# Narrowing the float64 weights: the middle bits as integers from ScalarE, sign and exponent placed in the upper half words by VectorE, the two added as integers by GpSimd

## The chip, the cores and the metric

One NeuronCore of a Trainium2 chip. TensorE (PE in the profile; PEld is its weight load) multiplies matrices into PSUM, VectorE (DVE), ScalarE (ACT) and GpSimd (POOL) work elementwise, SyncE (SP) issues the DMAs. The metric is the device time of one execution in microseconds, lower is better.

## The reference

Attention with four sink positions and a window of 128, in 4 batches of 8 heads, then a token mixer of rank 32 and a feed-forward network (FFN) with 2048 hidden units:

```python
keep = is_sink | in_window
scores = np.where(keep, scale * np.matmul(q, k.transpose(0, 1, 3, 2)), -1e9)
a = np.exp(scores - np.max(scores, axis=-1, keepdims=True))
a = a / (np.sum(a, axis=-1, keepdims=True) + 1e-09)
x = np.matmul(a, v)                      # then (B, H, S, D) -> (B, S, H * D)
u = x + (x.transpose(0, 2, 1) @ U @ V).transpose(0, 2, 1)
return u + np.maximum(u @ w_ch1, 0.0) @ w_ch2
```

q, k and v are float32 when they are multiplied. U, V, `w_ch1` and `w_ch2` reach the kernel as float64, 8 bytes an element, and have to be made float32 on the chip: 35 blocks of 128 partitions, one of 192 columns (U), two of 384 (V) and 32 of 512 (16 slices f of the hidden units, each with one block of `w_ch1` and one of `w_ch2`).

## The kernel before

A batch is attended in pairs of heads and halves of the sequence (`attend`): scores on PE (line 598), minimum and mask on DVE (605), exponential on ACT (608), normalisation on POOL or ACT, transposes (650), masked copies, values (680). The mixer follows (`mix_half`, `mix_end`): transposes (779), a product that shrinks to rank 32 (788), its copy `t` on ACT with a correction on DVE (829), then products that go back (842), whose results DVE adds to `xT` (844); `uh` and `ul` are the high and low part of the result, as the FFN reads them.

The FFN (`ffn`) takes one half of a batch, c, and a list of slices f. One step of it is 12 products of 384 columns (lines 868 to 870), the ReLU on ACT (876), its low part `hl` on DVE (879) and 9 products of 512 columns (889). Four batches of two halves and 16 slices make 128 steps. Batch 0 goes through the slices in groups of four, each for one half and then for the other (`spread`), since the slices are narrowed on the way; attention of the next batch is mixed into each batch's FFN.

`narrow` makes one block float32. A raw block `raw` (tile `big`, a ring of four that the FFN's outputs use too) is loaded by DMA. `narrow_steps` then takes, per element, the top 16 bits (`top`) and the 32 bits below (`mid`). Line 90 or 91 (DVE or ACT) drops the sign, 92 clamps the exponent, 93 or 94 (DVE or ACT) shifts it to that of float32, 95 puts the sign back: `a` is the upper half of the float32, read as bfloat16. Line 96 keeps sign and exponent in `s`, 97 multiplies `mid` by 2^-36 and by `s`, 98 adds the two. For the weights, 97 and 98 write a PSUM bank (`BANKED`), which releases the raw block after line 97. `weights` then copies the sum to the rounded high part of `w` (lines 458 and 459, ACT or DVE) and takes the rest as the low part (465, DVE alone when banked). A step of the FFN needs all four parts of its slice.

`Plan` decides order and engine of all of this before the program is written: steps with several `ways` are given an engine by a forward pass over assumed costs and due times, in which work of DVE and POOL that is marked to use their common port excludes each other. The result is one fixed order for each engine, and each engine takes its instructions in that order and waits at the one whose operand is not there.

Of the kernel before, what the change touches and what calls it, by code (L numbers as in the profile page):

```python
# [21 lines left out]
P = 128  # L22
# [28 lines left out]
NNR = 6  # L51
# [11 lines left out]
BANKED = True  # L63
# [7 lines left out]
def f32(ap):  # L71
    return ap.bitcast(F32)
# [6 lines left out]
def narrow_steps(nc, raw, n, a, s, x=None):  # L79


    x = x or (lambda: f32(raw())[:, 1:2 * n + 1:2])
# [16 lines left out]
          "POOL": lambda: g.tensor_tensor(x(), ab(), x(), ALU.add)}, "a", "raw"),  # L99
    ]  # L100
# [314 lines left out]
def dve(n):  # L415
    return 0.069 + n * 1.042e-3
# [14 lines left out]
class Fast:  # L431
# [44 lines left out]
    def narrow(self, src, n, prio, dst=()):  # L476

        raw, A, S_ = self.raw(), self.nr(), self.nr()
        if len(self.early) > 0:
            self.early.pop(0)  # L480
        else:
            self.put(raw, lambda: (raw().bitcast(U16)[:, 1:4 * n + 1], src), P * n * 8, prio - 8.0)
        x = self.bank() if dst else None
        box = {"raw": raw, "a": A, "s": S_}
        cost = (0.069 + n * 0.52e-3, 0.069 + n * 0.26e-3, 0.069 + n * 0.26e-3, dve(n), 0.069 + n * 0.26e-3, dve(n), dve(n))
        steps = narrow_steps(self.nc, raw, n, lambda: A()[:, :n], lambda: S_()[:, :n], x and (lambda: x()[:, :n]))
        for i, ((ways, r, w), c) in enumerate(zip(steps, cost)):
            r, w = (box[r],) if r else (), box[w]
            if x and i >= 5:
                r, w = r + (w,), x  # L490
                if i == 5:
                    r += tuple(dst)
                else:
                    ways = {"DVE": ways["DVE"]}
            self.plan.any({e: (c if e == "DVE" else gps(n) if e == "POOL" else act(n) + 0.09, fn, e != "ACT" and not (x and i == 6))
                           for e, fn in ways.items()}, r=r, w=(w,), prio=prio)
        if x:
            return x, lambda: x()[:, :n]
        return raw, lambda: f32(raw())[:, 1:2 * n + 1:2]
# [33 lines left out]
    def weights(self, f, prio):  # L533

        if f in STREAMED:
            i, w = self.slot()
            self.held[f] = (i, w)
            self.recent.append(f)
        else:
            w = self.w[f] = Box(lambda i=len(self.w): self.wtiles[i])  # L540
        for j, src in enumerate((self.w1[f], self.w2[f])):
            tb, tw = self.narrow(src, DM, prio, ((w, 2 * j), (w, 2 * j + 1)) if BANKED else ())
            hi, lo = (lambda i=i: w()[:, i, :] for i in (2 * j, 2 * j + 1))
            self.copy(DM, hi, tw, psum=BANKED, r=(tb,), w=((w, 2 * j),), prio=prio)
            self.tt(DM, lo, tw, lambda hi=hi: f32(hi()), ALU.subtract, pool=not BANKED,
                    r=(tb, (w, 2 * j)), w=((w, 2 * j + 1),), prio=prio)
        if f in STREAMED:
            wd = self.wd[f]
            self.put(wd, lambda: (f32(wd()), f32(w())), 1 << 20, prio, r=(w,))
        return w  # L550
# [398 lines left out]
    def run(self):  # L949
# [8 lines left out]
        self.wtiles, self.banks, self.bigs, self.accs, tiles = [], [], list(self.early), [], []  # L958
        bigs = Ring(NBIG, None)
        self.raw, self.big = self.share(bigs, self.bigs, lambda t: t), self.share(bigs, self.bigs, lambda t: f32(t[:, :DM]))  # L960
        self.nr = ring(NNR, [P, DM], U16, "nr")
        flat = [list(pair) for pair in self.first]
# [54 lines left out]
        for i in range(NP):  # L1017
            tiles.append(self.pool.tile([P, 2, NBLK, SW + SW], F32, name=f"p{i}"))
        with tc.manual_schedule():
            for s in order:  # L1020
                s.fn()
# [240 lines left out]
```

## Time and profile before

| | |
|---|---|
| runs shown | 756.87, 757.01, 757.60 us, median 757.01 us |
| profiled execution | 756.17 us, its span 754.4 us |
| PE busy | 728.8 us, 97% of the span |
| DVE busy | 387.6 us, 51% |
| ACT busy | 319.1 us, 42% |
| POOL busy | 125.9 us, 17% |
| mean granted TensorE clock | 0.994 of full speed |

Busy shares are means over the whole span. Matmuls overlap in the records, so that a PE that is 97% busy may still run below its rate; the 40 slices, the tables by stretch and the start times of equal steps tell more. Everything of the narrowing lies before 240 us.

### The profile page before, as it was taken

How to read it: one execution, taken by the hardware profiler on the slowest of the kernel's cores; microseconds unless marked ns; L12 is line 12 of the kernel's file. 1: busy time of each engine (PE TensorE's matmuls, PEld its weight loads, DVE VectorE, ACT ScalarE, POOL GpSimd, SP SyncE). 2: the span in 40 equal slices, each digit the busy share in tenths (PEclk: the TensorE clock that was granted, in tenths of full speed). 3: DMA queues.
4: the chain of work that ended last, by engine and by line, in shares of the span. 5: the costliest groups of instructions: out<-in, count | busy, mean ns of one | idle time of the engine just before them, and what ended most of it. 6: DMA issues, size and time to landing. Idle time of an engine off the chain costs nothing.

```text
span 754.4 us, 11107 instructions
## 1 busy us (share of the span) xinstructions
PE 728.8 (97%) x4004; PEld 604.8 (80%) x4004; DVE 387.6 (51%) x1044; ACT 319.1 (42%) x898; POOL 125.9 (17%) x194
## 2 busy tenths in 40 slices
PE   7987899999999999999999999999999999999996
PEld 5556777778787887787899977877889999999995
DVE  7999899898999524235551163242651131112111
ACT  6876475774863436245521164362641111111110
POOL 4742020321312122023120030120310000000000
PEclk9999999999999999999999999999999999999999
DMA  8565767666684366542465446431256527524752
GB/s 280 167 204 206 280 233 237 244 223 231 215 297 165 126 208 209 188 176 74 159 212 197 163 156 215 168 112 56 94 176 239 214 92 263 185 106 132 261 186 94
DMA packets 39103, 140.41 MB, mean 186 GB/s; under 512 B 4352, under 2 KB 8064, under 8 KB 29568
## 3 DMA queue, kind: packets, MB, share of 16 engines
q1 hardware_dynamic: 38752, 139.23, 52.7%
q8 instruction: 33, 0.54, 0.3%
q10 hardware_dynamic: 288, 0.39, 0.2%
q14 instruction: 30, 0.25, 0.1%
HBM read 109.98 MB, written 29.62 MB: 185 GB/s over the span
## 4 chain that ended last, share of the span: by engine, by line
PE 77%; DVE 16%; ACT 3%; issue 1%; DMA 1%; DVEq 0%; ACTq 0%; SPq 0%
PE bank L889 31%; PE bank L868 11%; PE bank L869 10%; PE bank L870 10%; PE bank L598 5%; PE bank L680 3%; DVE nr L95 2%; PE bank L650 2%; DVE bank L97 2%; DVE p L605 2%; DVE w L465 1%; DVE oph L656 1%; ACT p L608 1%; DVE xT L844 1%; DVE bank L98 1%
## 5 line engine op out<-in xcount | busy, mean ns | idle before, releaser
L889 PE MATMUL bank<-w,hh 128*128 128x512 f32 x768 | 244.3, 399 | 1.9 <-DVE w L465 1.3
L879 DVE SCALAR_TENSOR_TENSOR hl<-bank,hh 128x384 fp32r<-128x384 f32 x128 | 71.1, 555 | 270.5 <-ACT hh L876 270.0
L876 ACT ACTIVATE hh<-bank 128x384 fp32r<-128x384 f32 x125 | 61.4, 491 | 277.8 <-PE bank L870 277.2
L868 PE MATMUL bank<-ul,w 128*128 128x384 f32 x512 | 177.7, 347 | 1.1 <-ACT w L458 0.3
L869 PE MATMUL bank<-uh,w 128*128 128x384 f32 x512 | 172.3, 337 | 0.7 <-DVE w L465 0.7
L870 PE MATMUL bank<-uh,w 128*128 128x384 f32 x512 | 172.1, 336 | 0.0
L889 PEld LDWEIGHTS bank<-w,hh 128*128 128x128 f32 x768 | 140.1, 189 | 30.8 <-issue 5.7
L889 PE MATMUL bank<-w,hl 128*128 128x512 f32 x384 | 152.2, 396 | 1.6 <-DVE hl L879 1.6
L868 PEld LDWEIGHTS bank<-ul,w 128*128 128x128 f32 x512 | 96.0, 188 | 19.2 <-issue 10.8
L608 ACT ACTIVATE p<-p,mn 128x260 f32<-128x260 f32 (+1 forms) x192 | 92.8, 486 | 25.9 <-DVE mn L605 24.6
L869 PEld LDWEIGHTS bank<-uh,w 128*128 128x128 f32 x512 | 96.2, 188 | 6.9 <-DVE w L465 1.8
L870 PEld LDWEIGHTS bank<-uh,w 128*128 128x128 f32 x512 | 96.1, 188 | 0.0
L889 PEld LDWEIGHTS bank<-w,hl 128*128 128x128 f32 x384 | 72.5, 189 | 18.6 <-DVE hl L879 3.1
L605 DVE CUSTOM_DVE_ANT_0 p<-bank,mask 128x260 f32<-128x260 f32 (+1 forms) x192 | 68.2, 401 | 23.7 <-PE bank L598 23.3
L467 POOL TENSOR_TENSOR p<-p 128x256 f32<-128x256 f32 (+1 forms) x34 | 29.3, 871 | 218.1 <-ACT p L608 215.6
L598 PE MATMUL bank<-kp,qp 64*128 64x260 f32 (+1 forms) x360 | 55.4, 405 | 2.3 <-DVE p L465 1.2
L598 PEld LDWEIGHTS bank<-kp,qp 64*128 64x128 f32 x360 | 30.3, 188 | 19.7 <-DVE mn L605 10.6
L680 PE MATMUL bank<-oph,vp 128*64 128x256 f32 (+1 forms) x448 | 45.4, 340 | 0.0
L680 PEld LDWEIGHTS bank<-oph,vp 128*64 128x64 f32 x448 | 28.4, 136 | 18.0 <-issue 6.9
L467 POOL TENSOR_TENSOR ul<-xT,uh 128x384 fp32r<-128x384 f32 x15 | 15.6, 1062 | 159.0 <-ACT uh L458 113.5
L660 POOL TENSOR_SCALAR_AFFINE_SELECT oph<-oph 128x384 f32<-128x384 f32 x64 | 34.0, 550 | 36.7 <-ACT oph L458 36.4
L608 ACT ACTIVATION_READ_ACCUMULATOR p<-p,mn 128x1 f32 x192 | 36.4, 190 | 0.0
(144 smaller groups left out, 697.7 us busy)
## 6 DMA issues: line engine op xcount, KB each, us to landing
w<-wd SPq DMA_DIRECT2D x60, 1024.0 KB, 4.8
big<-in_w_dram SPq DMA_DIRECT2D x32, 512.0 KB, 4.2
wd<-w SPq DMA_DIRECT2D x14, 1024.0 KB, 4.4
big<-xd SPq DMA_DIRECT2D x33, 256.0 KB, 2.8
out_dram<-big SPq DMA_DIRECT2D x24, 256.0 KB, 2.1
kp<-in_k_dram SPq DMA_DIRECT2D x12, 396.0 KB, 3.3
qp<-in_q_dram SPq DMA_DIRECT2D x12, 384.0 KB, 4.3
vp<-in_v_dram SPq DMA_DIRECT2D x12, 384.0 KB, 4.0
```

Source lines behind the costliest of these rows:

```text
L467: ways["POOL"] = (gps(n), lambda: nc.gpsimd.tensor_tensor(dst(), a(), b(), op), True)
L598: nc.tensor.matmul(st()[:, :wd], qr()[rows, q0:q0 + P], kr()[rows, k0:k0 + wd], start=True, stop=True)
L605: add("DVE", dve(wd), lambda st=st, row=row, at=at, lo=lo, wd=wd, qb=qb: nc.vector.tensor_tensor_reduce(row(), st()[:, :wd], self.mask[:, ...
L608: add("ACT", act(wd) + 0.22, lambda row=row, at=at: nc.scalar.activation(row(), row(), AF.Exp, bias=at(mn), scale=-1.0, accum_out=at(sm)), ...
L660: add("POOL", 0.126 + CH * 0.914e-3, lambda: nc.gpsimd.affine_select(top(), top(), [[0, NBLK], [1, P]], ALU.is_ge, 0.0, base=0, channel_mu ...
L680: nc.tensor.matmul(pa()[i * D:(i + 1) * D, c0 * P:(c0 + hi - lo) * P], vr()[:, i, kb - kb0, :], mv, start=n == 0, stop=n == len(mms) - 1, ...
L868: nc.tensor.matmul(ph()[:, :CH], wh, ul()[:, d, :], start=d == 0, stop=False)
L869: nc.tensor.matmul(ph()[:, :CH], wl, uh()[:, d, :], start=False, stop=False)
L870: nc.tensor.matmul(ph()[:, :CH], wh, uh()[:, d, :], start=False, stop=d == NC - 1)
L876: self.plan.any({"ACT": (act(CH), lambda: nc.scalar.activation(hh(), ph()[:, :CH], AF.Relu)), "DVE": (dve(CH), lambda: nc.vector.tensor_sc ...
L879: add("DVE", dve(CH), lambda: nc.vector.scalar_tensor_tensor(hl(), ph()[:, :CH], 0.0, f32(hh()), ALU.max, ALU.subtract), r=(ph, hh), w=(hl ...
L889: nc.tensor.matmul(acc[k](), a()[:, sl], w()[:, m, :], start=not begin and i == 0 and j == 0, stop=i == n - 1 and j == 2)
```

## The change

The weights, U and V are narrowed by `join_steps`. The steps that drop the sign, clamp and shift the exponent stay (new lines 112 to 117). The middle 32 bits are turned into a rounded integer by ACT alone (new line 114, in place in the raw block), line 118 writes sign and exponent into the upper halves of 32-bit words of a new tile `nt`, whose lower halves are zero from the start (two memsets), and POOL alone adds the two as 32-bit integers (line 119) into the raw block: its words are then the float32. Lines 96 to 98 are gone. The PSUM bank is no longer used, so that the high part is now copied from the raw block, and the low part may be taken by POOL as well as by DVE; the raw block is released only after that. `nr` has two buffers and not six, `nt` has two.

```diff
-NNR = 6
+NNR = 2
+NNT = 2
-BANKED = True
+def join_steps(nc, raw, n, a, t):
+
+    x = lambda: words(raw())[:, 1:2 * n + 1:2]
+    mid = lambda: raw().bitcast(U32)[:, 1:2 * n + 1:2]
+    top = lambda: raw().bitcast(U16)[:, 4:4 * n + 4:4]
+    topb = lambda: raw().bitcast(BF16)[:, 4:4 * n + 4:4]
+    ab = lambda: a().bitcast(BF16)
+    high = lambda: t().bitcast(U16)[:, 1:2 * n:2]
+    v = nc.vector
+    return [
+        {"DVE": lambda: v.tensor_scalar(a(), top(), 0x7FFF, None, ALU.bitwise_and),
+          "ACT": lambda: nc.scalar.activation(ab(), topb(), AF.Abs)},
+        {"ACT": lambda: nc.scalar.activation(x(), mid(), AF.Copy, scale=2.0 ** -13)},
+        {"DVE": lambda: v.tensor_scalar(ab(), ab(), TOP_MIN, TOP_MAX, ALU.max, ALU.min)},
+        {"DVE": lambda: v.tensor_scalar(a(), a(), 14336.0, 8.0, ALU.subtract, ALU.mult),
+          "ACT": lambda: nc.scalar.activation(a(), a(), AF.Copy, bias=-114688.0, scale=8.0)},
+        {"DVE": lambda: v.scalar_tensor_tensor(high(), top(), 0x8000, a(), ALU.bitwise_and, ALU.bitwise_or)},
+        {"POOL": lambda: nc.gpsimd.tensor_tensor(x(), words(t())[:, :n], x(), ALU.add)},
     ]
...
     def narrow(self, src, n, prio, dst=()):
-        raw, A, S_ = self.raw(), self.nr(), self.nr()
+        raw, A, T = self.raw(), self.nr(), self.nt()
...
+        top, mid = (raw, "t"), (raw, "m")
+        steps = join_steps(self.nc, raw, n, lambda: A()[:, :n], T)
+        use = (((top,), A), ((), mid), ((), A), ((), A), ((top, A), T), ((T,), mid))
...
-            tb, tw = self.narrow(src, DM, prio, ((w, 2 * j), (w, 2 * j + 1)) if BANKED else ())
+            tb, tw = self.narrow(src, DM, prio)
             hi, lo = (lambda i=i: w()[:, i, :] for i in (2 * j, 2 * j + 1))
-            self.copy(DM, hi, tw, psum=BANKED, r=(tb,), w=((w, 2 * j),), prio=prio)
-            self.tt(DM, lo, tw, lambda hi=hi: f32(hi()), ALU.subtract, pool=not BANKED,
+            self.copy(DM, hi, tw, r=(tb,), w=((w, 2 * j),), prio=prio)
+            self.tt(DM, lo, tw, lambda hi=hi: f32(hi()), ALU.subtract,
                     r=(tb, (w, 2 * j)), w=((w, 2 * j + 1),), prio=prio)
...
+            for t in joins:
+                nc.gpsimd.memset(t, 0)
```

The plan gives every engine another order. Over the whole program PE and SP have the same instructions as before. On DVE the instructions of lines 96, 97 and 98 (35, 35 and 34) are gone, that of line 95 is line 118 now, and of the 32 low parts of `w` 25 are left. ACT has 35 of line 114, POOL 35 of line 119 and 7 low parts of `w`.

On DVE, just ahead of the correction of the mixer's `t` (line 829 before, 840 now; `pst` is a small product of the mixer, `w0` and `w2` the first slices, `big` raw blocks, `nr` and `nt` their halves), there stood these; ten more of line 92 to 98 and others stood above them, back to the row of `pst`:

```order
L465 TENSOR_TENSOR w0_166<-bank2_160,w0_166 128x512
L92 TENSOR_SCALAR nr_770<-nr_770 128x512
L97 SCALAR_TENSOR_TENSOR bank6_164<-big0_89,nr_768 128x512
L93 TENSOR_SCALAR nr_770<-nr_770 128x512
L98 TENSOR_TENSOR bank6_164<-nr_751,bank6_164 128x512
L95 SCALAR_TENSOR_TENSOR nr_770<-big1_91,nr_770 128x512
L96 TENSOR_SCALAR nr_800<-nr_770 128x512
L465 TENSOR_TENSOR w0_166<-bank6_164,w0_166 128x512
L97 SCALAR_TENSOR_TENSOR bank7_165<-big1_91,nr_800 128x512
L92 TENSOR_SCALAR nr_802<-nr_802 128x512
L98 TENSOR_TENSOR bank7_165<-nr_770,bank7_165 128x512
L829 TENSOR_TENSOR t_807<-bank4_162,t_807 32x512
```

Now there stand only these between the row of `pst` (line 830) and the correction:

```order
L115 TENSOR_SCALAR nr_732<-nr_732 128x512
L485 TENSOR_TENSOR vst_436<-big2_93,vst_436 32x384
L118 SCALAR_TENSOR_TENSOR nt0_175<-big0_89,nr_716 128x512
L485 TENSOR_TENSOR xhl_757<-bank3_161,xhl_757 64x384
L118 SCALAR_TENSOR_TENSOR nt1_176<-big1_91,nr_732 128x512
L485 TENSOR_TENSOR w0_166<-big3_95,w0_166 128x512
L485 TENSOR_TENSOR w0_166<-big0_89,w0_166 128x512
L115 TENSOR_SCALAR nr_796<-nr_796 128x512
L116 TENSOR_SCALAR nr_796<-nr_796 128x512
L840 TENSOR_TENSOR t_798<-bank6_164,t_798 32x512
```

The work ahead of the correction has become half as many instructions, and the low parts of `w0` read the raw block in SBUF where they read a PSUM bank.

On POOL, from the last masked copy of batch 0's attention (`oph`) to the low parts of the mixer's result (`ul`), there stood:

```order
L660 AFFINE_SELECT oph_657<-oph_657 128x3x128
L660 AFFINE_SELECT oph_704<-oph_704 128x3x128
L660 AFFINE_SELECT oph_707<-oph_707 128x3x128
L467 TENSOR_TENSOR ul_839<-xT_380,uh_830 128x384
L467 TENSOR_TENSOR ul_849<-xT_380,uh_837 128x384
```

In the same place there stands now:

```order
L671 AFFINE_SELECT oph_712<-oph_712 128x3x128
L119 TENSOR_TENSOR big2_93<-nt0_175,big2_93 128x384
L119 TENSOR_TENSOR big3_95<-nt1_176,big3_95 128x512
L119 TENSOR_TENSOR big0_89<-nt0_175,big0_89 128x512
L119 TENSOR_TENSOR big1_91<-nt1_176,big1_91 128x512
L487 TENSOR_TENSOR w2_168<-big1_91,w2_168 128x512
L487 TENSOR_TENSOR ul_827<-xT_351,uh_818 128x384
L487 TENSOR_TENSOR ul_839<-xT_351,uh_825 128x384
L119 TENSOR_TENSOR big2_93<-nt0_175,big2_93 128x512
```

Four integer additions and one low part of `w2` have come between, and more follow behind the two rows of `ul`.

On ACT, between the mixer's `t` and the first ReLU (line 876 before, 887 now), the eight copies to `uh` stood in one piece, behind one instruction of line 94 and one copy to `w2`. Now five copies to `uh` stand higher up and one behind the ReLU, and directly ahead of the ReLU there are:

```order
L114 ACTIVATE big3_95<-big3_95 128x512
L478 CAST uh_818<-xT_427 128x384
L113 ACTIVATE nr_861<-big0_89 128x512
L478 CAST uh_818<-xT_494 128x384
L114 ACTIVATE big0_89<-big0_89 128x512
L117 ACTIVATE nr_832<-nr_832 128x512
L887 ACTIVATE hh_882<-bank3_161 128x384
```

The conversions of `mid` to integers stand among the copies that the FFN's first products read.

## Rows read from the trace of the kernel before

**Rows 1.** The page: span, busy by engine, DVE in 40 equal slices (tenths).
```profile
span 754.4 us, 11107 instructions
PE 728.8 (97%) x4004; PEld 604.8 (80%) x4004; DVE 387.6 (51%) x1044; ACT 319.1 (42%) x898; POOL 125.9 (17%) x194
DVE  7999899898999524235551163242651131112111
```
**Rows 2.** By stretch: its length, then busy PE, PEld, DVE, ACT, POOL; clock; DMA.
```profile
20.00:40.00 20.00, 18.12 (x135) 11.92 (x133) 19.58 (x76) 18.34 (x70) 14.68 (x22) 1.00 0.57 189
...
40.00:68.10 28.10, 21.77 (x135) 13.97 (x131) 26.72 (x58) 20.08 (x53) 8.88 (x13) 1.00 0.70 233
68.10:90.00 21.90, 19.11 (x87) 15.36 (x88) 19.84 (x37) 10.59 (x20) 3.50 (x3) 1.00 0.54 189
...
40.00:240.00 200.00, 187.57 (x1036) 146.82 (x1033) 183.22 (x437) 127.01 (x327) 42.46 (x57) 0.99 0.66 229
240.00:754.00 514.00, 508.32 (x2754) 434.86 (x2753) 169.92 (x454) 160.38 (x454) 60.02 (x93) 1.00 0.47 166
```
**Rows 3.** Line 868 alone by stretch: 128 products of it are 32 FFN steps.
```profile
68.10:257.20 189.10, 45.40 (x128) 24.20 (x129) 0.99 0.63 222
257.20:435.00 177.80, 44.58 (x128) 24.00 (x128) 1.00 0.50 174
435.00:614.00 179.00, 44.77 (x128) 23.99 (x128) 1.00 0.43 151
```
**Rows 4.** The chain that ended last, 37.6 to 86 us, by line.
```profile
by line: DVE nr L95 13.9%; DVE bank L97 9.5%; DVE w L465 8.0%; DVE xT L844 7.7%; DVE nr L96 6.6%; DVE oph L656 5.9%; ACT nr L94 5.3%; DVE ul L465 5.2%; DVE bank L98 4.2%; DVE p L605 4.2%; DVE nr L92 3.8%; issue 3.4%; DVE big L98 2.8%; DVE v
```
**Rows 5.** DVE's groups by form: total busy us, mean ns of one, idle before.
```profile
L95 DVE SCALAR_TENSOR_TENSOR nr<-big,nr 128x512 uint16<-128x512 uint16 x32 | 24.0, 751 | 1.0
L97 DVE SCALAR_TENSOR_TENSOR bank<-big,nr 128x512 f32<-128x512 uint32 x32 | 22.2, 694 | 0.6
L98 DVE TENSOR_TENSOR bank<-nr,bank 128x512 f32<-128x512 bf16 x32 | 22.0, 689 | 0.3
L465 DVE TENSOR_TENSOR w<-bank,w 128x512 fp32r<-128x512 f32 x32 | 21.9, 683 | 2.7 <-ACT w L458 2.6
L96 DVE TENSOR_SCALAR nr<-nr 128x512 uint16<-128x512 uint16 x32 | 10.0, 311 | 0.3
```
**Rows 6.** ACT's groups by form.
```profile
L91 ACT ACTIVATE nr<-big 128x512 bf16<-128x512 bf16 x27 | 18.3, 676 | 4.6 <-DMA big<-in_w_dram 4.6
L458 ACT CAST w<-bank 128x512 fp32r<-128x512 f32 x31 | 18.2, 587 | 17.7 <-DVE bank L98 17.6
L94 ACT ACTIVATE nr<-nr 128x512 uint16<-128x512 uint16 x23 | 14.5, 631 | 24.6 <-DVE nr L92 24.6
```
**Rows 7.** POOL's groups by form that are nearest to the new addition.
```profile
L467 POOL TENSOR_TENSOR xhl<-first1q,xhl 128x512 fp32r<-128x512 f32 x3 | 3.9, 1294 | 25.1 <-ACT xhl L458 10.2 <-PE bank L801 8.5 <-DVE xhl L459 6.4
...
L99 POOL TENSOR_TENSOR big<-nr,big 128x192 f32<-128x192 bf16 x1 | 0.6, 556 | 0.0
```
**Rows 8.** ACT's timeline: the first and the fourth ReLU of the FFN.
```profile
71.61 0.49 ACT L876 ACTIVATE hh<-bank 128x384 fp32r<-128x384 f32 x1 [1.82 <-PE bank L870]
...
88.06 0.49 ACT L876 ACTIVATE hh<-bank 128x384 fp32r<-128x384 f32 x1
```
**Rows 9.** The chain in order of time: two FFN steps where PE waits for nothing.
```profile
589.36 2.06 PE bank L889 x9
593.51 2.06 PE bank L889 x9
```
**Rows 10.** POOL's timeline at 228 us: start, length, what.
```profile
228.68 2.97 POOL L467 TENSOR_TENSOR vsh<-first1k,vsh 32x512 fp32r<-32x512 f32 x2 [5.47 <-ACT vsh L458]
```
**Rows 11.** DVE's timeline beside it, and one instruction where POOL is idle.
```profile
228.71 1.80 DVE L95 SCALAR_TENSOR_TENSOR nr<-big,nr 128x512 uint16<-128x512 uint16 x1
...
255.00 0.56 DVE L465 TENSOR_TENSOR ul<-xT,uh 128x384 fp32r<-128x384 f32 x1
```

More of the change, by code (lines that the diff above doesn't have):

```diff
@@ L76, in words, with narrow_steps @@
     return ap.bitcast(I32)
-def narrow_steps(nc, raw, n, a, s, x=None):
-    x = x or (lambda: f32(raw())[:, 1:2 * n + 1:2])
+def narrow_steps(nc, raw, n, a, s):
+    x = lambda: f32(raw())[:, 1:2 * n + 1:2]
     mid = lambda: raw().bitcast(U32)[:, 1:2 * n + 1:2]
@@ L99, in narrow_steps @@
           "POOL": lambda: g.tensor_tensor(x(), ab(), x(), ALU.add)}, "a", "raw"),
+    ]
+def join_steps(nc, raw, n, a, t):
[15 more added lines that the diff above has]
+        {"POOL": lambda: nc.gpsimd.tensor_tensor(x(), words(t())[:, :n], x(), ALU.add)},
     ]
@@ L482, in narrow @@
             self.put(raw, lambda: (raw().bitcast(U16)[:, 1:4 * n + 1], src), P * n * 8, prio - 8.0)
[L483 to L495, printed above, removed]
+        top, mid = (raw, "t"), (raw, "m")
+        steps = join_steps(self.nc, raw, n, lambda: A()[:, :n], T)
+        use = (((top,), A), ((), mid), ((), A), ((), A), ((top, A), T), ((T,), mid))
+        cost = (0.069 + n * 0.52e-3, 0.0, 0.069 + n * 0.26e-3, 0.069 + n * 0.26e-3, dve(n), 0.0)
+        for ways, (r, w), c in zip(steps, use, cost):
+            self.plan.any({e: (c if e == "DVE" else gps(n) if e == "POOL" else act(n) + 0.09, fn, e != "ACT")
                            for e, fn in ways.items()}, r=r, w=(w,), prio=prio)
-        if x:
-            return x, lambda: x()[:, :n]
-        return raw, lambda: f32(raw())[:, 1:2 * n + 1:2]
+        return (raw, "m"), lambda: f32(raw())[:, 1:2 * n + 1:2]
     def mixers(self):
@@ L957, in run @@
         self.t = ring(2, [P, DM], F32R, "t")
-        self.wtiles, self.banks, self.bigs, self.accs, tiles = [], [], list(self.early), [], []
+        self.wtiles, self.banks, self.bigs, self.accs, tiles, joins = [], [], list(self.early), [], [], []
         bigs = Ring(NBIG, None)
@@ L961, in run @@
         self.nr = ring(NNR, [P, DM], U16, "nr")
+        self.nt = self.share(Ring(NNT, None), joins, lambda t: t)
         flat = [list(pair) for pair in self.first]
@@ L1018, in run @@
             tiles.append(self.pool.tile([P, 2, NBLK, SW + SW], F32, name=f"p{i}"))
+        joins += [self.pool.tile([P, DM], I32, name=f"nt{i}") for i in range(NNT)]
         with tc.manual_schedule():
+            for t in joins:
+                nc.gpsimd.memset(t, 0)
             for s in order:
```

## The prediction

> **What bounds the kernel now.** The page comes first: PE is busy 97% of the span and DVE 51%, but the slices show DVE at 9 tenths in the first third and at 1 to 3 later [rows 1]. So the share of the whole says nothing of the part where the weights are narrowed. The table by stretch puts it in numbers: from 40 to 240 us DVE is busy 183.2 of 200, ACT 127.0, POOL 42.5; after 240 us DVE 169.9 of 514 [rows 2]. All narrowing lies in that first stretch.
>
> Since busy PE may be slow PE, I take equal work instead. Thirty-two FFN steps are 128 products of line 868. Those of batch 0, with attention of batch 1 between them, take 189.1 us; those of batches 1 and 2, each with the attention of one batch between them, 177.8 and 179.0, mean 178.4 [rows 3]. The other difference is the narrowing. So 10.7 us are lost inside batch 0's FFN, and that is most of what a better narrowing can return there; about 1.4 of it I set aside for six products of 512 columns that only batch 0's FFN has (0.23 each, 2.06 over 9 in [rows 9]), which leaves 9.3.
>
> Where are they? An FFN step that waits for nothing takes 4.15 us (593.51 less 589.36) [rows 9]. The first and the fourth ReLU of batch 0 are 16.45 us apart, three steps, which are 12.45 at that rate [rows 8]. So 4.0 us go in the first burst, and 5.3 in the other three groups of slices. The third place is ahead of the FFN. The chain that ended last runs on DVE almost without a break from 37.6 to 86 us, and the narrowing's lines 95, 97, 96 and 98 lead it with the mixer's own additions (844) among them [rows 4]: the FFN, which starts at 68.1, waits for a mixer that stands in DVE's queue behind the narrowing.
>
> **The change, part by part.** *DVE.* Lines 96, 97 and 98 go: 10.0 + 22.2 + 22.0 = 54.2 us for the 32 blocks [rows 5]. Line 118 costs what 95 does; it writes every second half word, which no row shows, and I take line 95's price, which is near the 0.69 of lines 97 and 98 (its 24.0 us over 32 include some delayed ones); bounds 0.6 and 0.9. Of 32 low parts 25 stay (less 4.8). DVE gets nine more exponent shifts at about 0.3, five copies to `w` and five ReLUs, at most 0.7 each: about 8. Together DVE has some 51 us less to do, 183 becomes about 132.
>
> *ACT.* 32 conversions of `mid`. The nearest rows are ACT's other passes over such a block: 0.631 from line 94, 0.676 from line 91 with a strided source [rows 6]. I take 0.65, bounds 0.55 (the step when they follow each other closely) and 0.75. That is 21 us, less nine shifts (5.7) and ten copies and ReLUs that DVE takes (about 5.4), with the smaller blocks about 11 more: 127 becomes 138 of 200. That alone bounds nothing.
>
> *POOL.* 35 integer additions and 7 low parts. The nearest row is a subtraction of 512 columns at 1.294; 192 columns of the old line 99, in the same strided block, took 0.556, which by columns gives the same [rows 7]. An integer addition is not in the trace: bounds 0.9 and 2.0, and I take 1.29. 32 + 7 at 1.29 and 2.4 for the three smaller ones are 53 us: 42.5 becomes 95 of 200. The two memsets stand ahead of POOL's first work, which waits for DVE's masks anyway.
>
> *The price that comes with it.* DVE's instruction of line 95 that started at 228.71 took 1.80 us. POOL's pair began at 228.68 and its first ended 1.28 later; DVE came to its end 0.55 us after that [rows 10, 11]. A subtraction of `ul` took 0.56 where POOL did nothing [rows 11]. So a DVE instruction that works in SBUF alone waits until POOL's is over. Those that read PSUM (97, 98, 465 as it was) kept to 0.69 throughout. The change removes just the unaffected ones and doubles POOL's time. About 145 such DVE instructions are left before 240 us (32 times the clamp, line 118 and most low parts, 21 shifts, some 40 of mixer and attention). At a POOL busy 95 of 200 us, nearly every second meets one, and half of about 1 us is lost each time: some 35 us. DVE ends near 132 + 35 = 167, still under 183.
>
> This is what the Trainium skill, "GPSIMD Engine Reference", section 8 (Key points), says: VectorE and GpSimd share SBUF interfaces, and instructions with two SBUF inputs or in a two-port mode contend. The low part of `w` had one SBUF input and has two now, so that by this rule the change moves work from the free kind to the contending one; the trace agrees (0.56 against 1.80 with POOL busy).
>
> *Moved work.* Between `pst` and the correction of `t`, DVE had 21 instructions, 14 of the kinds at 0.55 to 0.7 and 7 at 0.3, some 11 us by [rows 5]; the new order has nine, 6 and 3, some 5 us. The 6 us don't all come back, since `t` itself is made by ACT: ACT is busy 20.1 of the 28.1 us from 40 to 68.1 [rows 2]. Ahead of that the first conversions lengthen a stretch in which it has no room, 18.3 of 20 us [rows 2]. In all, by the first ReLU it has six conversions of 512 columns and three smaller ones more, about 5, less a few copies: 4 of its 8 idle us are filled. Half of what is left I give to the start of the FFN: 2.5 us earlier, bounds 0 and 5.
>
> *First burst.* At the first `hl` five blocks have passed line 118, where four had passed 95; three are left for three steps. In the time that DVE's SBUF work and POOL have to share, one block costs 0.3 (clamp) + 0.17 (shift, in 18 of 32) + 0.69 (line 118) + 0.54 (low part, in 25) + 0.08 (copy, in 6) on DVE and 1.29 + 0.28 on POOL, together 3.05 us, and with a meeting's loss of 0.3 some 3.35. Three blocks are 10 us, within the 12.45 of three steps. So the burst should lose little: 3.5 of 4.0 come back.
>
> *The other groups.* 24 blocks in the remaining 167 us are 7 us each, but they come in bursts, since a slot of `w` comes free only as an old slice has been used, and raw blocks are held until the low part is taken instead of until line 97. At 3.35 a block against steps of 5.9 us (189.1 over 32) for two blocks, the shared time is a little too short where blocks are wanted in a row, and there is room elsewhere. I take half of 5.3: 2.7 back.
>
> *Sum.* 2.5 + 3.5 + 2.7 = 8.7 us off the profiled 756.17 us: 747.5. The median of the runs is 757.01, 0.84 above that execution, so 748.3.
>
> **Rivals.** *A, the FFN starts no earlier and ACT is the next to be late.* The conversions now stand among the copies to `uh` that the first products read, and ACT is over 9 tenths busy in batch 0's attention [rows 2]. Against: 8 idle us before the FFN. Then only the bursts gain, 3 to 4 us: 753.
>
> *B, nothing is won.* The low part now needs ACT's conversion, POOL's addition and ACT's copy in turn, with `nr` and `nt` two deep and the raw block held longer. If each block takes as long as the 3.5 us that DVE needed (0.75 + 0.31 + 0.69 + 0.69 + 0.68 by [rows 5], some 0.4 for clamp and shift), the wait for line 98 becomes one for 119: 757.
>
> *C, slower: DVE stands still behind POOL.* In the shared time alone 32 blocks at 3.35 are 107 us where 32 of clamp, line 95 and line 96 were about 45; with POOL's 42 and some 20 of other DVE work that is 169 of 200. It decides when DVE is held during more than 51 of POOL's 95 us, over half; then DVE's 132 is above 183 again. At three quarters it is 71, 20 too many, of which PE would see about half, since its own steps cover the rest: 767. For it: the order is fixed, so that a held DVE also holds masks and `hl`. Against: line 95 took 0.75 on average with POOL busy a fifth of the time, only 9% over its own. The rule of the Trainium skill just named would lead here if every addition met a DVE instruction.
>
> *D, all is won:* 9.3 and 5, so 743.
>
> **Chances.** The forecast, 748 (745 to 751), 0.45; D 0.08; A 0.20; B 0.09; C 0.18. The range of 8 in 10 goes from D to B's upper end, 742 to 758, and leaves out C and little else. The likeliest case's own range is the 745 to 751 given with it. Within 0.2% (1.5 us, about what this kernel's runs can tell apart) lies B and a bit of A: same 0.10; faster 0.45 + 0.08 + 0.19 = 0.72; slower 0.18.
>
> **What the profile of the changed kernel would show.** Right: 128 products of line 868 in batch 0 in about 183 us; the first at 65 to 66; the first to fourth ReLU in 13 us; DVE 20 to 50 us less busy in all, POOL near 179, ACT near 330; POOL's addition at 1.2 to 1.4 us. The chain from 40 to 86 should show ACT and POOL beside DVE. Wrong: line 118 or the low part of `w` at a mean of 1 us or more (C); PE waiting for POOL's line 119 or ACT's copies of `w` in the bursts (B); the first product of the FFN at 68 or later (A). An addition of 2 us would make a block 4.1 us of shared time and turn the sum round.

## The result, and the profile of the changed kernel

The changed kernel takes 749.17 us (median of 4 runs, 748.03 to 750.35) against 756.94 us beside it: ratio 0.99, 95% interval 0.9877 to 0.9924. It is 7.8 us faster; 8.7 had been forecast. Its profiled execution took 748.03 us, with a span of 746.3, 8.1 less than the span in [rows 1].

The page: span, busy time by engine and DVE's 40 slices.

```profile
span 746.3 us, 11090 instructions
...
PE 725.6 (97%) x4004; PEld 604.3 (81%) x4004; DVE 357.1 (48%) x949; ACT 326.8 (44%) x910; POOL 182.8 (24%) x242
...
DVE  7889787776886614426541253243651131112112
```

The table by stretch, columns as in [rows 2]:

```profile
40.00:240.00 200.00, 191.48 (x1082) 153.42 (x1081) 160.99 (x358) 137.82 (x347) 98.04 (x101) 1.00 0.68 239
240.00:746.00 506.00, 500.91 (x2717) 428.12 (x2715) 164.46 (x445) 157.25 (x447) 58.87 (x92) 1.00 0.47 166
```

DVE went from 183.2 to 161.0 of 200 us and POOL from 42.5 to 98.0, and nearly all that changed lies ahead of 250 us. Line 879 (868 before), 128 products to a row, answers to [rows 3]:

```profile
66.10:249.80 183.70, 44.79 (x128) 24.03 (x129) 1.00 0.65 229
249.80:427.60 177.80, 44.58 (x128) 24.00 (x128) 1.00 0.49 174
427.60:606.70 179.10, 44.81 (x129) 24.01 (x128) 1.00 0.43 151
```

The first product comes at 66.1 instead of 68.1, batch 0's FFN takes 183.7 instead of 189.1, the other batches take what they took. That is 7.4 of the 8.1 us; another 0.8 lie behind the last step of batch 2 and were not followed.

Inside batch 0's FFN I now cut where the fifth step's first product starts. Before, then after the change, all engines by stretch:

```profile
68.10:87.80 19.70, 16.91 (x75) 13.24 (x76) 18.69 (x35) 9.88 (x19) 3.50 (x3) 1.00 0.50 174
87.80:257.20 169.40, 166.09 (x912) 135.09 (x912) 146.35 (x360) 102.22 (x268) 32.13 (x44) 0.99 0.64 227
```

```profile
66.10:86.00 19.90, 15.71 (x76) 13.16 (x76) 17.18 (x24) 12.12 (x24) 8.31 (x6) 1.00 0.58 187
86.00:249.80 163.80, 162.77 (x913) 134.06 (x912) 123.41 (x296) 106.93 (x274) 73.18 (x76) 1.00 0.66 235
```

PE does the same work in each pair (75 or 76 instructions, then 912 or 913), so the lengths can be compared. The first four steps won nothing: 19.7 before, 19.9 after. PE stands still for 4.2 us of them, where it stood still for 2.8 before; its busy time fell by 1.2 us at the same clock, for a reason that no row shows. The other 28 won 5.6 us, and PE stands still in them for only 1.0 us. The ReLUs of [rows 8] say the same of the first burst, 16.25 us between them instead of 16.45:

```profile
70.04 0.47 ACT L887 ACTIVATE hh<-bank 128x384 fp32r<-128x384 f32 x1
...
86.29 0.49 ACT L887 ACTIVATE hh<-bank 128x384 fp32r<-128x384 f32 x1 [2.49 <-PE bank L881]
```

The new and the kept groups by form (busy us, mean ns, idle before):

```profile
L119 POOL TENSOR_TENSOR big<-nt,big 128x512 int32<-128x512 int32 x32 | 43.6, 1364 | 57.1 <-DVE nt L118 45.3 <-ACT nr L113 6.1 <-DMA big<-in_w_dram 2.2
L118 DVE SCALAR_TENSOR_TENSOR nt<-big,nr 128x512 uint16<-128x512 uint16 x32 | 25.6, 802 | 2.3 <-ACT nr L117 1.4 <-issue 0.6
L485 DVE TENSOR_TENSOR w<-big,w 128x512 fp32r<-128x512 f32 x25 | 22.8, 914 | 1.6 <-ACT w L478 1.6
L115 DVE TENSOR_SCALAR nr<-nr 128x512 bf16<-128x512 bf16 x32 | 14.3, 450 | 6.8 <-ACT nr L113 6.7
```

The low part of `w` rose from 0.683 [rows 5] to 0.914 us and the clamp takes 0.450: DVE does stand behind POOL, though for less time than was reckoned.

Last, PE's standstills of more than 0.15 us in the first four steps, from its timeline (start, length, operation, in brackets the idle time and who ended it):

```profile
68.61 0.44 PE L879 MATMUL bank<-ul,w 128*128 128x384 f32 x1 [0.72 <-DVE ul L485]
...
76.22 0.51 PE L900 MATMUL bank<-w,hl 128*128 128x512 f32 x1 [2.19 <-DVE hl L890]
...
81.37 0.73 PE L900 MATMUL bank<-w,hh 128*128 128x512 f32 x2 [1.18 <-ACT hh L887]
```

DVE's timeline has what stood ahead of the `hl` that ended the longest:

```profile
71.32 1.29 DVE L115 TENSOR_SCALAR nr<-nr 128x512 bf16<-128x512 bf16 x1
72.54 1.67 DVE L485 TENSOR_TENSOR ul<-xT,uh 128x384 fp32r<-128x384 f32 x1
...
75.62 0.55 DVE L890 SCALAR_TENSOR_TENSOR hl<-bank,hh 128x384 fp32r<-128x384 f32 x1
```

The ReLU for that `hl` had ended at 72.4. DVE came to it at 75.6, after six others, among them a clamp of 1.29 us and a `ul` of 1.67 that take 0.29 and 0.55 where POOL is idle. There is another candidate in the same stretch. ACT's timeline has the copy of the fourth block:

```profile
70.41 0.65 ACT L478 CAST w<-big 128x512 fp32r<-128x512 f32 x1
```

The chain that ended last goes on from it to POOL's low part and a load:

```profile
71.14 1.33 POOL w L487
...
72.49 4.54 DMA big<-in_w_dram
```

That copy starts at 70.41, though POOL's sum was done at 68.14; only when POOL has taken the low part does the raw block come free, and the load that waits for it lands at 77.0. The last of the three standstills leads to the same load: the third ReLU stands on ACT behind lines 113, 114 and 117 of the block that it brings, and line 117 waits 1.38 us for a clamp that DVE makes at 79.99, behind a low part of 1.70 us.

### The profile page after: what moved, and what is told of

Same layout as the page of the kernel before. It is cut to its first block, busy times and chain, and to the rows that moved or that the text cites. A ratio compares the mean times of both kernels' runs of the same rounds, so it can differ in the third digit from the quotient of the medians.

```text
span 746.3 us, 11090 instructions
## 1 busy us (share of the span) xinstructions
PE 725.6 (97%) x4004; PEld 604.3 (81%) x4004; DVE 357.1 (48%) x949; ACT 326.8 (44%) x910; POOL 182.8 (24%) x242
## 4 chain that ended last, share of the span: by engine, by line
PE 85%; DVE 5%; ACT 4%; DMA 2%; POOL 2%; issue 1%; DVEq 0%; ACTq 0%; POOLq 0%
PE bank L900 34%; PE bank L879 13%; PE bank L881 11%; PE bank L880 11%; PE bank L609 5%; PE bank L691 4%; PE bank L661 2%; DMA big<-in_w_dram 2%; PE bank L790 1%; ACT p L619 1%; ACT oph L478 1%; DVE nt L118 1%; DVE p L616 1%; PE bank L917 1%; PE bank L853 1%
## 5 line engine op out<-in xcount | busy, mean ns | idle before, releaser
L887 ACT ACTIVATE hh<-bank 128x384 fp32r<-128x384 f32 x120 | 58.6, 488 | 278.3 <-PE bank L881 275.2
L616 DVE CUSTOM_DVE_ANT_0 p<-bank,mask 128x260 f32<-128x260 f32 (+1 forms) x192 | 68.1, 400 | 25.9 <-PE bank L609 25.6
L119 POOL TENSOR_TENSOR big<-nt,big 128x512 int32<-128x512 int32 (+2 forms) x35 | 46.3, 1323 | 60.1 <-DVE nt L118 45.3
L691 PE MATMUL bank<-oph,vp 128*64 128x256 f32 (+1 forms) x448 | 46.9, 341 | 2.0 <-POOL oph L671 2.0
L487 POOL TENSOR_TENSOR ul<-xT,uh 128x384 fp32r<-128x384 f32 x13 | 13.0, 1017 | 138.8 <-ACT uh L478 83.1
```

The source lines that it names most:

```text
L119: {"POOL": lambda: nc.gpsimd.tensor_tensor(x(), words(t())[:, :n], x(), ALU.add)},
L487: ways["POOL"] = (gps(n), lambda: nc.gpsimd.tensor_tensor(dst(), a(), b(), op), True)
L616: add("DVE", dve(wd), lambda st=st, row=row, at=at, lo=lo, wd=wd, qb=qb: nc.vector.tensor_tensor_reduce(row(), st()[:, :wd], self.mask[:, ...
L691: nc.tensor.matmul(pa()[i * D:(i + 1) * D, c0 * P:(c0 + hi - lo) * P], vr()[:, i, kb - kb0, :], mv, start=n == 0, stop=n == len(mms) - 1, ...
L887: self.plan.any({"ACT": (act(CH), lambda: nc.scalar.activation(hh(), ph()[:, :CH], AF.Relu)), "DVE": (dve(CH), lambda: nc.vector.tensor_sc ...
```

## The experiments

Four theories were put to the test. **Theory 1**: DVE's relief pays in the later groups, and in the first burst a raw block, held until the low part is taken, holds up the next load. **Theory 2**: the meetings of DVE and POOL in SBUF are what is left. **Theory 3**: it is not the integers but only the freedom to share with POOL that pays. **Theory 4**: ACT is late now. "Before" ran beside each: 755.3 to 755.5 us.

### DVE's relief alone

In the kernel before, in the same order, lines 96 and 98 emit nothing for the blocks of `w`, and line 97 reads `a` where it read `s`:

```diff
...
+            if x and i in (4, 6):
+                ways = {e: lambda: None for e in ways}
```

> The kernel before with all instructions in the same order, but lines 96 and 98 left out for the 32 blocks of w (the mask of the high half word and the addition of the sign part are left out, so w has other values). DVE has 32 us less to do and nothing is given to POOL or ACT; raw blocks and banks are held as before. If the relief of DVE is the gain: batch 0's FFN 5 to 9 us shorter (180 to 184) and the FFN's start 1 to 4 us earlier, 744 to 750. If DVE's queue was not what held PE: 755 to 757.

Measured: 750.09 us, ratio 0.993 (0.9912 to 0.9948). The same two stretches and DVE's table row:

```profile
67.30:86.00 18.70, 16.70 (x75) 13.04 (x76) 15.11 (x26) 9.78 (x19) 3.52 (x3) 1.00 0.54 185
86.00:251.60 165.60, 163.39 (x913) 134.23 (x912) 126.18 (x311) 100.86 (x267) 32.27 (x44) 1.00 0.65 232
...
40.00:240.00 200.00, 190.43 (x1067) 150.99 (x1064) 162.18 (x381) 127.86 (x333) 43.78 (x58) 1.00 0.66 236
```

With nothing given to POOL or ACT, 5.4 us of the change's 7.8 are there, and DVE has the load that it has after the change (162 us, 161). In the profiled execution 3.8 us lie in the last 28 steps: 1.1 are standstill, 2.7 are in PE's busy time, where the kernel before ran for 3.4 us at half clock (a row further down). So DVE's work in the narrowing was what held PE, for most of what the change won. The two lines are also links in the way of each block to its copy, and ACT's waits for the sum fell with them from 17.6 to 6.4 us: the run doesn't tell DVE's load from the length of that way.

### Sharing with POOL, without the integers

The kernel before with its seven steps, but the sum kept in the raw block, so that line 98 and the low part may go to POOL:

```diff
-BANKED = True
+BANKED = False
```

> The kernel before with its old seven steps, but without the bank of PSUM: the float sum stays in the raw block, and the addition of line 98 and the low part of w may go to POOL as in the changed kernel. Theory 1: DVE keeps lines 96 and 97 and most of its load, and raw blocks are held longer as well, so nothing is won: 756 to 765, with DVE above 170 us busy between 40 and 240. Theory 3 (it is only the sharing with POOL, not the integers, that pays): 747 to 752.

Measured: 757.3 us, ratio 1.0025 (1.0015 to 1.0035). Line 868 of batch 0:

```profile
67.70:257.10 189.40, 45.28 (x129) 24.20 (x129) 1.00 0.64 221
```

189.4 against 189.1 in [rows 3]: no gain, and the time is a little longer. The plan, which has another order here, gave POOL 8 low parts of `w` and 3 additions, and DVE was as busy as before (184.6 us from 40 to 240). Theory 3 falls: the freedom to share gave nothing, as the plan used it.

### POOL's additions taken away, and doubled

```diff
+            if n == DM and "POOL" in ways:
+                ways = {"POOL": lambda: None}
```

> The changed kernel in the same order, with the integer additions on GpSimd left out for the 32 blocks of w (w gets the converted low bits alone), so 41 us of POOL go and with them most meetings with DVE. Theory 2 (meetings are what is left of the loss): DVE's line 118 and low parts fall to 0.75 and 0.69, batch 0's FFN 4 to 6 us shorter, 741 to 745. Theory 1: a raw block is held 1.3 to 2 us less, so the first burst gains 1 to 2 us, and the rest 1 to 2: 745 to 748.

Measured: 749.42 us, ratio 0.9907 (0.9888 to 0.9925), the changed kernel's time, where both theories had forecast a gain. The two stretches again:

```profile
68.20:86.00 17.80, 15.48 (x77) 13.29 (x76) 12.34 (x24) 10.77 (x21) 1.32 (x1) 1.00 0.57 199
86.00:249.80 163.80, 162.64 (x913) 133.76 (x912) 114.83 (x296) 106.08 (x274) 40.45 (x52) 1.00 0.67 234
```

From 86.0 to 249.8 PE needs the same 163.8 us, though DVE is 8.6 and POOL 32.7 us less busy there. So from the fifth step on the meetings cost nothing, and theory 2 falls for that part. In the first four steps PE stands still 2.3 us instead of 4.2, but the FFN began 2.1 us later, behind a stretch (63.4 to 66.9) at a granted clock of 0.56, mostly the lower level of 1.2 GHz; both kernels reach the fifth step at 86.0. The chain that ended last goes through the same low part and load as in the changed kernel, a little over one us later:

```profile
72.29 1.33 POOL w L487
...
73.64 4.44 DMA big<-in_w_dram
```

How much of the first burst the meetings take can't be read from this run.

The other way, one more POOL instruction behind each addition:

```diff
-        {"POOL": lambda: nc.gpsimd.tensor_tensor(x(), words(t())[:, :n], x(), ALU.add)},
+        {"POOL": lambda: (nc.gpsimd.tensor_tensor(x(), words(t())[:, :n], x(), ALU.add),
+                          nc.gpsimd.tensor_tensor(f32(raw())[:, 1:2*n+1:2], f32(raw())[:, 1:2*n+1:2], f32(raw())[:, 1:2*n+1:2], ALU.add))},
```

> The changed kernel in the same order, with a second addition on GpSimd behind each integer addition (the narrowed value added to itself, so that it comes out doubled), 35 more of about 1.3 us, 44 us of POOL. The prediction said that an addition of 2 us, let alone 2.6, would turn its sum round. Theory 2: line 118 and the low parts meet POOL nearly always, batch 0's FFN 10 us longer or more, 758 to 770. Theory 1: each raw block is held 1.3 us longer in every burst, 752 to 757. If POOL has room: within 2 us of the changed kernel, as leaving the additions out gained nothing at the end.

Measured: 774.23 us, ratio 1.0242 (1.0227 to 1.0257), 25 us above the changed kernel for 42 more of POOL, and more than either theory forecast. By stretch:

```profile
71.20:94.10 22.90, 17.44 (x77) 14.21 (x76) 20.41 (x24) 11.11 (x21) 14.89 (x11) 0.93 0.43 149
94.10:273.70 179.60, 168.88 (x914) 134.90 (x913) 133.70 (x296) 106.57 (x274) 102.47 (x100) 1.00 0.61 214
```

DVE's low part among the groups by form, and the longest wait from 40 to 240 us (engine, line, waited for: us, times, longest):

```profile
L486 DVE TENSOR_TENSOR w<-big,w 128x512 fp32r<-128x512 f32 x25 | 28.1, 1125 | 9.7 <-ACT w L479 9.3
```

The latter from the view of waits:

```profile
ACT w L479 <- POOL big L120: 32.3, 17, 3.1
```

The low part of `w` is at 1.125 us, and ACT's copies wait 32.3 us for POOL (7.0 in the changed kernel). So POOL's work is cheap at one addition to a block and dear at two. Whether by meetings is not shown: DVE loses some 12 us more behind POOL than in the changed kernel (an estimate, each instruction less the lower quartile of its form), while ACT waits 25 more for a sum that comes 1.24 us later on POOL.

### Raw blocks

One raw block less, in both kernels:

```diff
-NBIG = 4
+NBIG = 3
```

> The changed kernel with three raw blocks in the ring instead of four. Theory 1: the load in front of each block starts one block later, and each burst loses what three loads take; the first to fourth ReLU over 20 us, batch 0's FFN 5 to 15 us longer, 755 to 765, and a loss larger than that of the same edit in the kernel before. Theory 2 (meetings of DVE and POOL): the blocks pass the engines at the same rate, so within 3 us of the changed kernel, 747 to 752.

> The kernel before with three raw blocks instead of four; the partner of the run on the changed kernel. There the raw block is given back at line 97, some 4 us after line 95, not at the low part. Theory 1: it loses less than the changed kernel does, 1 to 6 us, 758 to 763. If raw blocks play no part: 757, as before. If it loses as much as the changed kernel, the longer hold is not what took the first burst's gain.

Measured: 765.98 us (1.0139, 1.0122 to 1.0156) and 761.73 us (1.007, 1.0049 to 1.0091). Batch 0's FFN by its first line of products, with three blocks in the changed kernel:

```profile
66.30:262.90 196.60, 45.87 (x128) 24.77 (x129) 0.98 0.62 216
```

And with three in the kernel before:

```profile
74.70:265.10 190.40, 45.84 (x128) 24.62 (x129) 0.99 0.60 211
```

The changed kernel loses 12.9 us inside the FFN; the kernel before loses 1.3 there, and 6.6 ahead of it (in both the edit also drops the fourth of the loads at the kernel's head). A longer hold would do this, but it is not isolated: both runs have plans of their own, with another order than with four blocks. Whether four are enough takes more blocks, for which SBUF has no room. The control gives up one resident slice of `w`:

```diff
-NRES = 2
+NRES = 1
...
```

> The changed kernel with one slice of w resident instead of two: slice 8 is stored and read back like the others, which frees the room of one slice. A control for the next run alone. Both theories: the stores and reads grow by one slice in each batch, which PE hides; 748 to 752, batch 0's FFN within 2 us of 183.6.

Measured: 746.17 us, ratio 0.9881 (0.9859 to 0.9902), below its forecast. By stretch:

```profile
68.90:84.40 15.50, 15.10 (x76) 13.16 (x75) 12.64 (x20) 8.09 (x15) 5.68 (x4) 1.00 0.53 195
84.40:247.80 163.40, 162.32 (x913) 134.01 (x912) 124.03 (x293) 109.94 (x282) 75.70 (x75) 1.00 0.69 242
```

This was meant as a control and became the main witness. But for the stores and reads of slice 8 the work is the same, and so is the number of raw blocks; the plan's order differs, and a few operations stand on another engine. The last 28 steps take what they took, but the first four take 15.5 us with 0.4 of standstill. The ReLUs are 12.54 us apart, the three dense steps of 12.45 that the prediction had reckoned:

```profile
72.16 0.49 ACT L887 ACTIVATE hh<-bank 128x384 fp32r<-128x384 f32 x1 [0.65 <-PE bank L881]
...
84.70 0.49 ACT L887 ACTIVATE hh<-bank 128x384 fp32r<-128x384 f32 x1 [2.44 <-PE bank L881]
```

In this order ACT makes the fourth copy of `w` at 63.92, ahead of the copies to `uh`, and POOL takes the low part at 64.65; in the changed kernel these stood at 70.41 and 71.14. ACT's timeline, then POOL's, of this run:

```profile
63.92 0.65 ACT L478 CAST w<-big 128x512 fp32r<-128x512 f32 x1
```

and

```profile
64.65 1.31 POOL L487 TENSOR_TENSOR w<-big,w 128x512 fp32r<-128x512 f32 x1 [1.04 <-ACT w L478]
```

So the raw block comes free sooner, and the last load of this burst is issued at 65.99; in the changed kernel it is the one that starts at 72.49:

```profile
65.99 0.33 SPq L493 DMA_DIRECT2D big<-in_w_dram  x1
```

The run begins the FFN later, though (68.9), behind four us near 1.2 GHz (0.59 from 64.8 to 68.9), so that its 746.17 us are no safe win over the changed kernel: the intervals overlap.

With the freed room, six raw blocks, first with an order made for six:

```diff
-NBIG = 4
+NBIG = 6
...
```

> The same as the run with one resident slice, and the room is used for six raw blocks instead of four (the two more are among the loads at the kernel's head). Theory 1 (a raw block, held until the low part of w is taken, holds up the next load): ACT's waits of line 113 for the load, 15.9 us of the stretch from 40 to 240, go below 5; first to fourth ReLU 12.5 to 14 us instead of 16.3; batch 0's FFN 3 to 8 us shorter than with four blocks; 741 to 746. Theory 2 (DVE and POOL meet too often): the blocks only wait at another place, batch 0's FFN within 2 us of the control, and the same time as the control within 2 us.

Measured: 752.1 us, ratio 0.9947 (0.9931 to 0.9964): slower than its control, which neither theory had, and batch 0's FFN takes 179.9 us against 178.9. PE loses nothing in the first four steps (16.60 of 16.60 us), but two more loads at the head and the new order bring the FFN's start to 74.0, where the control has 68.9, in part by 7.6 us ahead of it at a granted clock of 0.55:

```profile
74.00:90.60 16.60, 16.60 (x85) 15.10 (x85) 11.95 (x20) 7.54 (x15) 4.22 (x3) 1.00 0.52 162
```

Then with six blocks used in turn, in the control's exact order, so that only waits go:

```diff
-        return lambda: ring(lambda i=len(ring.boxes): view(tiles[i % ring.n]))
+        return lambda: ring(lambda i=len(ring.boxes): view(tiles[i % len(tiles)]))
...
```

> The run with one resident slice of w (control: e5), in exactly its order on every engine, but with six raw blocks in turn where the order was made for four; only waits are taken away. Theory 1: the load of a block no longer waits for the low part two or more blocks earlier; ACT's 12.9 us of waits for loads at line 113 go below 6, and batch 0's FFN, 178.9 in the control, gets 1 to 3 us shorter; 743 to 745. If the raw blocks hold nothing any more in that order: 745 to 747 and the same FFN within 0.5.

Measured: 747.82 us, ratio 0.9899 (0.9885 to 0.9913), an interval that overlaps the control's. By stretch:

```profile
68.00:84.30 16.30, 15.25 (x76) 13.32 (x77) 13.37 (x21) 8.78 (x17) 5.76 (x4) 1.00 0.60 212
84.30:246.60 162.30, 161.59 (x912) 133.94 (x912) 123.25 (x293) 110.55 (x282) 74.98 (x75) 1.00 0.66 239
```

Its waits from 40 to 240 us have this row:

```profile
ACT nr L113 <- DMA big<-in_w_dram: 3.8, 4, 1.5
```

ACT's waits for loads fell from 12.9 to 3.8 us, as theory 1 said, and PE got next to nothing for it: 178.6 us against 178.9. In this order four blocks are enough, and theory 1 fails. For the changed kernel's own order that is not shown: in the control the fourth low part is taken at 64.65 and the last load issued at 65.99, ahead of the first product, while in the changed kernel it is taken at 71.14, with a load behind it on the chain. Six blocks in that order were not tried.

### The low part of w on DVE alone

```diff
-            self.tt(DM, lo, tw, lambda hi=hi: f32(hi()), ALU.subtract,
+            self.tt(DM, lo, tw, lambda hi=hi: f32(hi()), ALU.subtract, pool=False,
```

> The changed kernel with the low part of w always on DVE instead of DVE or POOL (seven blocks go over). Theory 1 (in the first burst what holds is a raw block, kept until the low part is taken, and the load that can only then begin; elsewhere the relief of DVE pays): the block whose low part stood behind POOL's own addition comes free earlier, the first to fourth ReLU go from 16.3 to about 15 us, the rest stays: 747 to 749. Theory 2 (what is left is lost to DVE and POOL meeting in SBUF): POOL has 9 us less, DVE 5 more, so that some seven meetings go; batch 0's FFN comes out 1 to 2 us shorter all over, 747 to 748. Both agree nearly here; the place tells them apart. A loss of more than 2 us would speak for DVE as the engine that still decides.

Measured: 750.75 us, ratio 0.9929 (0.9912 to 0.9947), not below the changed kernel; both theories had forecast 747 to 749. The fourth low part is taken at 68.3 instead of 71.1, and the first and the fourth ReLU are 13.94 us apart instead of 16.25; yet PE waits 1.61 and 0.82 us for low parts of `w` on DVE, the FFN starts at 68.0, and its last 28 steps take 166.5 us instead of 163.8. The plan has another order here, so what POOL's seven low parts are worth is not isolated.

### One `hl` moved forward

The changed kernel's order, with the second `hl` five DVE instructions earlier:

```diff
...
+        s = sorted(self.hls, key=order.index)[1]
+        i = order.index(s)
+        at = [k for k, x in enumerate(order[:i]) if x.eng == "DVE"][-5]
+        order.insert(at, order.pop(i))
```

> The changed kernel in the same order, but for one DVE instruction: the second hl of the FFN goes ahead of two additions of ul, line 116, line 115 and line 118, to just behind the first hl and one line 115. In the changed kernel PE stood still 2.19 us for it (76.22) while DVE, in front of it, took 1.29 and 1.67 us for instructions of 0.28 and 0.55 beside POOL. Theory 2 (that delay of DVE beside POOL took the first burst's gain): the stall goes below 0.3, the fifth step's first product comes at 84 instead of 86.0, and about 2 us stay to the end: 746 to 748. Theory 1 (the raw block and its load, which landed at 77.0, hold the third step): the second step starts earlier, but PE waits for the low part of w instead, the fifth step at 85.5 to 86, and 748 to 750.

Measured: 749.68 us, ratio 0.9927 (0.9913 to 0.9941). PE's standstills from the second step on:

```profile
76.48 0.44 PE L879 MATMUL bank<-ul,w 128*128 128x384 f32 x1 [0.45 <-ACT w L478]
78.07 0.45 PE L880 MATMUL bank<-uh,w 128*128 128x384 f32 x1 [1.14 <-DVE w L485]
81.82 0.73 PE L900 MATMUL bank<-w,hh 128*128 128x512 f32 x2 [1.57 <-ACT hh L887]
```

The stretch that holds the last of them and the one behind it, with PE's busy time first and the clock third from the end:

```profile
80.00:83.00 3.00, 1.33 (x5) 0.59 (x4) 2.30 (x4) 1.56 (x3) 1.32 (x2) 1.00 0.96 309
83.00:87.00 4.00, 4.00 (x14) 3.44 (x13) 1.80 (x2) 0.67 (x1) 0.56 (x1) 0.57 0.76 247
```

The 2.19 us are gone and the third step starts 1.4 us earlier (76.5 for 77.9), but PE then waits for the fifth block. That is the wait that theory 1 named, though not for its reason: the fifth block's sum was done at 74.4, its copy stood on ACT behind a line 117 until 75.8, and its low part took 1.55 us beside POOL. A standstill of 1.57 follows, for the third ReLU behind a line 117 again, and behind it the clock is near its lower level for almost four us, so that the fifth step comes at 88.0, which neither theory had. One wait hid another, and curing the first alone gave nothing.

### ACT's conversion doubled

```diff
-        {"ACT": lambda: nc.scalar.activation(x(), mid(), AF.Copy, scale=2.0 ** -13)},
+        {"ACT": lambda: (nc.scalar.activation(x(), mid(), AF.Copy, scale=2.0 ** -13),
+                         nc.scalar.activation(x(), x(), AF.Copy))},
```

> The changed kernel in the same order, with a second pass of ACT over each converted block (integers to the same integers), 35 more of about 0.65 us, 21 us of ACT. Theory 4 (ACT is what is late now, the prediction's rival A): the FFN starts 2 us later or more and the bursts lose as well, 755 to 762. If ACT has the room that its 134 us of 192 suggest: within 2.5 us of the changed kernel, 748 to 752.

Measured: 757.8 us, ratio 1.0047 (1.0017 to 1.0078): all of the gain is gone for 21 us of ACT. By stretch:

```profile
68.30:89.80 21.50, 17.60 (x76) 14.20 (x75) 16.40 (x24) 14.48 (x27) 8.28 (x6) 0.92 0.54 175
89.80:259.20 169.40, 165.11 (x914) 134.34 (x913) 124.51 (x296) 120.66 (x298) 72.65 (x76) 1.00 0.64 226
```

So ACT, busy 138 of 200 us, has no free 21: the FFN starts 2.2 us later, its first four steps take 1.6 longer and the rest 5.6. Theory 4 is right in that ACT has little room left. The run does not show that ACT alone holds the first burst.

## Why the prediction came out nearly right, term by term

**The bound** was read rightly. Taking 32 us of DVE's work from the narrowing pays 5.4 us without any other edit. Of the 10.7 us that batch 0's FFN took longer than the others, 4.8 come back in that run and 5.4 in the changed kernel; where the other half goes is open.

**The prices** held. The conversion takes 0.678 us (0.65 said), the integer addition 1.364 (1.29), line 118 0.802 and 0.776 without the additions (line 95's 0.751 was to be its price; the sum of a block has 0.69). POOL came to 98 us of 200 (95), ACT to 138 (138), DVE to 161 (167). Of the 35 us that DVE was to lose behind POOL, 23.4 came true (36 instructions from 40 to 240 us, each less the lower quartile of its form, an estimate); taking the additions away gave back 14.7 of DVE's time (161.0, and 146.3 in that run). The share of meetings was set too high: some 72 instructions were to lose 0.5 us each, 36 lost 0.65.

**The FFN's start** came 1.9 us earlier by the first product (68.11 and 66.17), 2.5 said, bounds 0 and 5. That it comes from fewer DVE instructions ahead of `t` is not shown: DVE's relief alone gave 0.8, and the other plans began anywhere from 66.4 (three raw blocks, changed kernel) to 74.8 (three, kernel before).

**The first burst** is the step that failed. "Three blocks are 10 us, within the 12.45 of three steps. So the burst should lose little: 3.5 of 4.0 come back." Nothing came back (19.7 and 19.9 us). The sum of a block has a slip: its seven terms make 3.35 us and not 3.05, and 3.65 with a meeting's loss, so that three blocks are 11 us and rival C's 107 are 117. Eleven still fit within 12.45, and the rate was right as a capacity: with nearly the same work and the same ring, the order with one resident slice does three steps in 12.54. What failed is taking a rate for an order. In the changed kernel's order the fourth copy of `w` stands on ACT behind conversions, copies to `uh` and the first ReLU, and the second `hl` on DVE behind instructions that wait for ACT or for POOL. Which of these waits sets the fifth step is not settled: moving the `hl` uncovered the low part of `w`. The load behind the fourth low part, which starts 6.5 us earlier in the other order, is a candidate that no run takes away. Neither moving ACT's copy forward in that order nor six blocks in it was tried.

**The other groups** were mis-sized: 5.6 us came back (169.4 less 163.8), 2.7 said. Of these 2.3 are PE's standstill (3.3 to 1.0). Another 1.7 are the clock, by an estimate: half of 3.4 us. A stretch of the kernel before shows it: there PE ran 3.4 us at 1.2 GHz (0.50), about a standstill of 1.29 us on the low part of `w` that ended at 234.16:

```profile
233.80:237.20 3.40, 3.04 (x7) 2.49 (x8) 3.27 (x8) 1.19 (x2) 0.00 (x0) 0.50 0.74 258
```

The remaining 1.6 are in matmuls that the profile counts as busy (166.1 less 1.7 and 162.8). "The shared time is a little too short where blocks are wanted in a row" was wrong for these groups: taking the additions away changed nothing there. So two errors in size nearly cancelled, 3.7 us too much in the burst and 2.9 too little in the other groups; that the total came out so near is luck.

**The rivals.** A (no earlier start, ACT late): the start was earlier, but doubling ACT's conversions shows how near it stood. B: ACT's waits for the block's sum fell from 17.6 [rows 6] to 7.0, so line 119 is no second line 98; but its waits for loads rose from 4.6 [rows 6] to 15.9 with the longer hold, which costs PE nothing in the one order in which six blocks were tried against four. C: the mechanism is there and its price is not. The Trainium skill, "GPSIMD Engine Reference", section 8 (Key points), has VectorE and GpSimd contend for shared SBUF interfaces where a VectorE instruction has two SBUF inputs or runs in a 2-port mode. The trace agrees for two inputs (a `ul` of 1.67 where 0.55 is free); the clamp has one, took 1.29 where 0.29 is free, and no row shows its mode. The prediction set 1.80 beside 0.56, times of two different instructions; line 95 by itself takes 0.69. From the fifth step on PE gains nothing when the additions go. The prediction's own condition, an addition of 2 us, was not tried; at 2.6 (1.364 and 1.244) the sum did turn round. D: true of the later groups, not of the burst.

## What to carry to other kernels

Take work off the engine whose queue is the bound even if another engine then takes longer for it: 54 us of DVE were exchanged for 44 of POOL and 21 of ACT, with gain. Ask how much room those have left: the same again, on either of them, gave back all of the gain or more. A rate that fits says only that a burst can be dense; whether it is depends on where each copy and each `hl` stands in the fixed order, and this differs between two plans of nearly the same work by some 4 us of standstill. And look at a stretch's standstill and clock together: removing one wait is worth nothing if the next stands right behind it.

## What the runs showed of the hardware

An integer addition of 128x512 on GpSimd costs about what a float operation does: 1.364 us beside DVE's work, against 1.294 for the subtraction in [rows 7] and 1.244 for the float addition in the run with two, whose inputs lie in one strided block. ACT's second pass, from integers to integers, takes 0.679 us, and the conversion ahead of it 0.676.

The granted clock fell to its lower level for three to four us, in one run for 7.6, and twice the rows show PE busy only in part ahead of it: 1.33 of 3.00 us ahead of the stretch at 0.57, and in the kernel before 4.39 of 5.80 ahead of the one at 0.50. But the changed kernel had standstills of 2.19 and 1.18 us in its first burst and kept 1.00, so that the length of a standstill alone doesn't tell when it falls.
